# Folding the key weights in sixteen array tiles over 512 columns, put in place by DMAs through DRAM, in a gated mix of linear attention and a feed-forward layer

## The chip, the core and the metric

The kernel runs on one core of one Trainium2 chip. The metric is the device time of one execution in microseconds, the median of several runs. Before the change it is 508.11 us (three runs, 507.98 to 508.29).

## What is computed

One input x (2048 rows of 512) goes through two branches, which a gate mixes row by row. All values are float32.

```python
q, k, v = split(x @ wqkv)                  # 32 heads of 16
pq, pk = q @ w_phi, k @ w_phi              # w_phi: one 16x16 matrix per head
phi_q = [softmax(pq), softmax(-pq)];  phi_k = [softmax(pk), softmax(-pk)]
kv = phi_k^T v;  z = sum(phi_k)            # per head, over all rows
a = (phi_q kv) / (phi_q z + 1e-6) @ wo
b = relu(x @ w1 + b1)^2 @ w2 + b2          # w1: 512x1792
g = sigmoid(sum(x * gate_w))
out = g * a + (1 - g) * b
```

## The kernel before, in words

**Numbers.** Each float32 operand of a large matmul is split into a high part and a low part (`split`, L62: ScalarE copies the high part, L64, VectorE subtracts it for the low one, L67), and a product is three matmuls (`mm3`, L75: L77, L78, L79). So whoever wants a weight needs ScalarE first and VectorE second.

**The feed-forward branch** is the backbone of the order. The 1792 hidden columns are 14 chunks of 128, in two sweeps of seven (0 to 6, 7 to 13); each sweep runs over four blocks of 512 rows. For each chunk an up projection (12 matmuls) fills one PSUM bank `u`; ScalarE does the relu with bias into `r` (L418), the square (L419) and the high part `hh`; VectorE does the low part `hl`; twelve down matmuls add to four banks `d`. There are two buffers for `r`. Four further banks turn round (`bank`, L54): hidden tiles, folds and projections take the one that was used longest ago, and wait until it has been read. Two of them are taken out of the turn later, one for the sums over keys, one for `pX`.

**The attention branch** is laid between these steps. Every function of it has a slot, in half steps: slot 2t is before step t's up projection, 2t + 1 behind it, 2t + 1.5 in the midst of step t's down matmuls (`at`, L782, `run`, L843). The slots fix an order in which the code is recorded; a scheduler then orders the instructions of each engine, by priorities and its own estimates, and from there on every engine works through its row strictly from the front. What it chose is shown by the order of the built program.

**The key weights.** The product wk times w_phi is folded once into one matrix, since pk = x (wk w_phi). w_phi has 32 diagonal blocks of 16, so the fold works in array tiles of 32 by 32: `tiles_fold` (L177) does 64 matmuls over 128 columns (four `g`, four `c`, four row strips `r`) into four PSUM banks, VectorE turns the four banks by 32 by 32 blocks into two tiles `turned` (L196), and ScalarE copies them in 16 pieces to their places in four `raw` tiles (L200; two of them lie in one tile `tmp`), next to the value weights that a DMA has put there (L175). It is called at slot 5.5, in step 2, at the head of the first `joint` piece.

**What uses them.** Keys and values are projected together, with seven products in place of eight (a Strassen scheme over rows and columns). `joint` (L215), in six pieces at slots 5.5 to 11, makes from the `raw` tiles the weights of the products: `operand` (L203) splits one, and VectorE's subtractions (L216) between them make the next. Four are held in SBUF; three go through two slots (`sloto` 0 and 1) or others and are stored to DRAM (`wkeep`, L213) and fetched again later. Slot 0 is written with product 3's weights, stored, and then written with product 1's, which the first `pX` matmul reads at slot 14. `joint_last` (L233) makes the last two weights, `w4`.

**Loads.** SyncE issues the loads in its row; a DMA waits there for its buffer to be free. Eight completion counters turn round, so a DMA also waits for the one eight before it. The stage `in` has four buffers.

Of the kernel before, what the change touches and what calls it, by code (L numbers as in the profile page):

```python
# [8 lines left out]
F32 = mybir.dt.float32  # L9
F32R = mybir.dt.float32r  # L10
AF = mybir.ActivationFunctionType
# [5 lines left out]
P = 128  # L17
S, D, H, DH, F = 2048, 512, 32, 16, 1792
NK = D // P
# [10 lines left out]
AHEAD = 150  # L30
HELD = 2, 4, 5, 7
# [4 lines left out]
def tile_gated_mix(ctx: ExitStack, tc: tile.TileContext, xT, xn, wqT, wkT, wphi, wv, wo, w1, b1, w2, b2, gw, out):  # L36
    nc = tc.nc
# [83 lines left out]
    st, up_w, down_w = {}, {}, {}  # L121
# [9 lines left out]
    nc.gpsimd.memset(kvb, 0.0)  # L131
    part = dram.tile([NB * NC, P, D], F32, name="part")
    wkeep = dram.tile([len(KEPT), 2, P, 2 * D], F32, name="wkeep")
    zrow = dram.tile([2 * D], F32, name="zrow")
    vext = [hold.tile([P, H * VW], F32, tag="vz", name=f"vext{i}") for i in range(NV)]
    heads = lambda v: v.rearrange("p (h v) -> p h v", v=VW)
# [13 lines left out]
    def fold(loaded, nm, k):  # L150
        wph, *t = loaded
        ps = bank(f"fold{nm}{k}")
        for g in range(NK):
            nc.tensor.matmul(ps[:, g * P:(g + 1) * P], t[g][:, k * P:(k + 1) * P], wph[:, g * P:(g + 1) * P],
                             start=True, stop=True)
        hi = wpool.tile([P, 512], F32R, tag=f"wah{k}", name=f"w{nm}h{k}")
        lo = wpool.tile([P, 512], F32R, tag=f"wal{k}", name=f"w{nm}l{k}")
        with tc.high_priority(offset=AHEAD):
            split(ps, hi, lo, nc.scalar, nc.vector)
        return hi, lo  # L160
# [16 lines left out]
    def tiles_fold(loaded):  # L177
        wph, *t = loaded
        pss = [bank(f"fold{r}") for r in range(4)]

        def mm(g, r, c):
            rows, cols = slice(32 * r, 32 * r + 32), slice(32 * c, 32 * c + 32)
            return nc.tensor.matmul(pss[r][cols, g * P:(g + 1) * P],
                                    wph[rows, g * P + 32 * r:g * P + 32 * r + 32],
                                    t[g][rows, :].rearrange("p (k c q) -> p k c q", c=4, q=32)[:, :, c, :],
                                    start=True, stop=True, skip_group_check=True)

        last = None
        for x in [(g, r, c) for g in range(NK) for c in range(4) for r in range(4)]:
            with tc.issue_after(last.ins) if last else nullcontext():  # L190
                last = mm(*x)
        for half in range(2):
            tb = work.tile([P, 2, 4, NK, 32], F32, tag="tb", name="turned", bufs=2)
            for r in range(2):
                with tc.high_priority(offset=AHEAD):
                    st["turned"] = nc.vector.transpose(tb[:, r].rearrange("p g k q -> p (g k q)"), pss[2 * half + r])  # L196
            for k in range(NK):
                dst = st["raw"][k].rearrange("p (h z g r f) -> p h z g r f", h=2, z=2, g=2, r=4)
                for h in range(2):
                    nc.scalar.activation(dst[:, h, 0, :, 2 * half:2 * half + 2],  # L200
                                         tb[:, :, 2 * h:2 * h + 2, k].rearrange("p r g q -> p g r q"), AF.Copy)

    def operand(i, j, src, slot=None, ehi=None, elo=None):  # L203
        if i in HELD:
            w, k = "ab"[i > 4], 2 * (HELD.index(i) % 2) + j
            hi, lo = (wpool.tile([P, 512], F32R, tag=f"w{w}{hl}{k}", name=f"w{i}{j}", bufs=1) for hl in "hl")
# [248 lines left out]
    def do_fold(nm, k):  # L455
        with tc.issue_after(st["up"].ins):
            st["wa", nm, k] = fold(st["wT"], nm, k)
        if k == NK - 1:
            st["wa"] = [st["wa", nm, i] for i in range(NK)]
            if nm == "k":  # L460
                banks.pop()

    def do_joint(j, piece):
        if (j, piece) == (0, 0):
            joint_start(st["wT"])
            with tc.issue_after(st["up"].ins):
                tiles_fold(st["wT"])
        with tc.issue_after(st["up"].ins):
            joint(j, piece)
        if (j, piece) == (1, 0):  # L470
            banks.remove(ps_b)
# [310 lines left out]
    def at(slot, f, *a):  # L782
        steps.setdefault(int(2 * slot) / 2, []).append(lambda: f(*a))

    for fc in range(LAG + 1, NFH):
        if fc > FIRST:
            at(2 * (fc - LAG) - 2, do_w1_first, fc)
        at(2 * (fc - LAG) - (2 if fc == LAG + 1 else 1), do_w2, fc)
    at(0, do_wT, wkT)
    for slot, j, piece in ((5.5, 0, 0), (6, 1, 0), (8, 0, 1), (9, 1, 1), (10, 1, 2), (11, 0, 2)):  # L790
        at(slot, do_joint, j, piece)
    for j in range(2):
# [48 lines left out]
    hid, last = {}, len(work_list) - 1  # L841
# [107 lines left out]
```

## Time and profile before

| what | value |
|---|---|
| median of the runs | 508.11 us (507.98 to 508.29) |
| span of the profiled execution | 506.8 us |
| TensorE busy | 502.0 us, 99% |
| VectorE busy | 405.9 us, 80% |
| ScalarE busy | 256.2 us, 51% |
| GpSimd busy | 88.4 us, 17% |
| DMA | 76.13 MB, 150 GB/s in the mean |
| the fold's matmuls (L183) | start at 27.00 us |
| the fold's four transposes (L196) | start at 28.88 us |
| first `pX` matmul (L647) | 52.31 us |

The span is the time from the first to the last instruction of one execution; the runs' times hold a little more. In a row of the profile, "L77 PE MATMUL d<-w2h,hh 128*128 128x512 f32 x222 | 86.9, 391" is line, engine, operation, tile written and tiles read, shape, count, busy us in all and mean ns of one; behind it stands the idle time of the engine ahead of such instructions, and who ended it. Matmuls overlap in a pipeline: one lasts 390 ns, and the next starts long before its end. L-numbers are those of the kernel before; behind the changed lines the change's numbers are 1 to 6 higher.

### The profile page before, as it was taken

What the parts mean: (1) busy time and instruction counts of PE and PEld (TensorE: products, weight loads), DVE (VectorE), ACT (ScalarE), POOL (GpSimd) and SP (SyncE); (2) the same over time, 40 slices, a digit from 0 to 9 for tenths busy, and PEclk for the clock granted to TensorE, in tenths of its full rate; (3) what the DMA queues carried; (4) which work ended last, traced back from release to release, by engine and by line L of the source; (5) the groups of instructions that cost most, each with busy time, mean ns of one, the idle gap of its engine ahead of it and who ended that gap; (6) DMA issues with size and microseconds to landing.
All of it is one profiled execution on the core that took longest, in us unless ns stands there. A gap on an engine that the chain in (4) does not pass through costs nothing.

```text
span 506.8 us, 9362 instructions
## 1 busy us (share of the span) xinstructions
PE 502.0 (99%) x3522; PEld 406.4 (80%) x3522; DVE 405.9 (80%) x679; ACT 256.2 (51%) x458; POOL 88.4 (17%) x103
## 2 busy tenths in 40 slices
PE   9999999999999999999999999999999999999997
PEld 5878788788888888888888877788787878788776
DVE  5569957998795979796898989897869797897824
ACT  4887655555263474454574745444456354333540
POOL 0000151204420025000013050211222221111200
PEclk9999999999999999999999999999999999999999
DMA  8858587756854578771375221325112231032102
GB/s 262 279 194 284 187 311 219 232 196 231 288 187 158 182 236 308 242 228 65 87 219 195 63 83 43 104 76 147 39 31 88 71 85 43 8 125 63 38 26 84
DMA packets 45861, 76.13 MB, mean 150 GB/s; under 512 B 6904, under 2 KB 23032, under 8 KB 45816
## 3 DMA queue, kind: packets, MB, share of 16 engines
q1 hardware_dynamic: 36104, 41.78, 26.7%
q10 hardware_dynamic: 6768, 23.79, 13.7%
q0 software_dynamic: 2944, 9.96, 5.4%
q8 instruction: 28, 0.46, 0.4%
q14 instruction: 17, 0.14, 0.1%
HBM read 57.68 MB, written 11.54 MB: 137 GB/s over the span
## 4 chain that ended last, share of the span: by engine, by line
PE 90%; DVE 6%; DMA 1%; POOL 1%; ACT 1%; issue 1%; DVEq 0%; POOLq 0%; ACTq 0%
PE d L77 9%; PE d L78 9%; PE d L79 9%; PE u L77 9%; PE u L78 8%; PE u L79 8%; PE pX L647 3%; PE att L79 3%; PE pX L649 3%; PE att L77 3%; PE att L78 3%; PE pX L648 3%; PE q L79 2%; PE q L78 2%; PE q L77 2%; PE pY L647 2%
## 5 line engine op out<-in xcount | busy, mean ns | idle before, releaser
L418 ACT ACTIVATE r<-u,b1c 128x512 f32<-128x512 f32 x56 | 38.5, 688 | 125.5 <-PE u L79 123.6
L77 PE MATMUL d<-w2h,hh 128*128 128x512 f32 x222 | 86.9, 391 | 0.0
L78 PE MATMUL d<-w2l,hh 128*128 128x512 f32 x222 | 86.5, 390 | 0.0
L79 PE MATMUL d<-w2h,hl 128*128 128x512 f32 x222 | 86.4, 389 | 0.0
L77 PE MATMUL u<-xh,w1h 128*128 128x512 f32 x212 | 83.7, 395 | 0.0
L78 PE MATMUL u<-xl,w1h 128*128 128x512 f32 x212 | 82.6, 390 | 0.0
L79 PE MATMUL u<-xh,w1l 128*128 128x512 f32 x212 | 82.5, 389 | 0.0
L333 POOL TENSOR_TENSOR ez<-e,z 128x512 f32<-128x512 f32 x32 | 43.1, 1370 | 166.6 <-ACT e L305 166.6
L67 DVE TENSOR_TENSOR hl<-r,hh 128x512 fp32r<-128x512 f32 x56 | 37.7, 674 | 24.7 <-ACT hh L64 24.7
L77 PEld LDWEIGHTS d<-w2h,hh 128*128 128x128 f32 x222 | 41.7, 188 | 9.2 <-issue 0.6
L78 PEld LDWEIGHTS d<-w2l,hh 128*128 128x128 f32 x222 | 41.7, 188 | 8.9 <-DVE w2l L67 0.4
L77 PEld LDWEIGHTS u<-xh,w1h 128*128 128x128 f32 x212 | 39.8, 188 | 11.1 <-issue 2.9
L79 PEld LDWEIGHTS d<-w2h,hl 128*128 128x128 f32 x222 | 41.7, 188 | 8.7
L79 PEld LDWEIGHTS u<-xh,w1l 128*128 128x128 f32 x212 | 39.8, 188 | 8.6 <-DVE w1l L67 0.2
L78 PEld LDWEIGHTS u<-xl,w1h 128*128 128x128 f32 x212 | 39.8, 188 | 7.9
L305 ACT ACTIVATE e<-e 128x1024 f32<-128x1024 f32 x27 | 28.6, 1059 | 25.2 <-DVE e L303 25.0
L308 DVE TENSOR_REDUCE sm<-e 128x64 f32<-128x1024 f32 x27 | 32.8, 1214 | 10.4 <-ACT e L305 10.4
L64 ACT ACTIVATE hh<-r 128x512 fp32r<-128x512 f32 x56 | 35.2, 628 | 1.1
L419 ACT ACTIVATE r<-r 128x512 f32<-128x512 f32 x56 | 35.0, 624 | 0.7
L686 ACT ACTIVATE tmp<-pX 128x512 f32<-128x512 f32 x24 | 14.4, 598 | 31.2 <-PE pX L649 27.6
L371 ACT ACTIVATE phiT<-tb 32x256 f32<-32x256 f32 x64 | 26.4, 412 | 6.1 <-DVE tb L356 5.1
L340 DVE TENSOR_REDUCE dz<-ez 128x64 f32<-128x1024 f32 x16 | 19.4, 1211 | 11.5 <-POOL ez L333 11.5
(184 smaller groups left out, 985.5 us busy)
## 6 DMA issues: line engine op xcount, KB each, us to landing
sloto<-wkeep ACTq DMA_DIRECT2D x30, 512.0 KB, 4.1
in<-in_xT SPq DMA_DIRECT2D x42, 256.0 KB, 4.2
slotez<-wkeep ACTq DMA_DIRECT2D x15, 512.0 KB, 4.6
phiT<-tb SPq DMA_DIRECT2D x192, 32.0 KB, 1.9
in<-in_w SPq DMA_DIRECT2D x23, 256.0 KB, 3.2
part<-row POOLq DMA_DIRECT2D x16, 256.0 KB, 5.2
row<-part SPq DMA_DIRECT2D x16, 256.0 KB, 2.7
out<-row SPq DMA_DIRECT2D x15, 256.0 KB, 2.2
```

The costliest lines, as they stand in the source:

```text
L64: i = nc.scalar.activation(hi, src, AF.Copy)
L67: st["lo"] = elo.tensor_tensor(lo, src, hi.bitcast(F32), ALU.subtract)
L77: nc.tensor.matmul(o, ah[:, sa], bh[:, sb], start=first, stop=False)
L78: nc.tensor.matmul(o, ah[:, sa], bl[:, sb], start=False, stop=False)
L79: return nc.tensor.matmul(o, al[:, sa], bh[:, sb], start=False, stop=last)
L305: nc.scalar.activation(ef, ef, AF.Exp)
L308: nc.vector.tensor_reduce(sm, e3, AX.X, ALU.add)
L333: nc.gpsimd.tensor_tensor(ez[:, hs, :], e3[:, hs, :], zbc[half], ALU.mult)
L371: nc.scalar.activation(dst, src, AF.Copy)
L418: st["relu"] = nc.scalar.activation(r, ps, AF.Relu, bias=b1c[:, fc:fc + 1])
L419: nc.scalar.activation(r, r, AF.Square)
L647: nc.tensor.matmul(ps, h, wh, start=first and j == 0, stop=False, skip_group_check=True)
```

## The change

The fold takes 16 matmuls instead of 64: for each strip `r` and each `g` one array tile goes over all 512 columns, so that the column strips of the array are now the four `g` and no longer the four `c`. It is called at slot 3.5, in step 1, instead of 5.5 (the value weights' DMAs and the tiles of `joint_start` come there too). VectorE turns the four banks into one tile `turned`, which shares its place in SBUF with the held weights `w4`. ScalarE's 16 copies are gone: four DMAs of 32 partitions each, in pieces of 128 numbers, store the turned tile to a DRAM tensor `wfold`, and four DMAs load it from there into the `raw` tiles. These eight are on SyncE's queue. The held weights of `w4` and the second half of the query weights now lie in one tile (`held`).

```diff
+    wfold = dram.tile([NK, P, D], F32, name="wfold")
...
     def tiles_fold(loaded):
         wph, *t = loaded
         pss = [bank(f"fold{r}") for r in range(4)]
-        def mm(g, r, c):
-            rows, cols = slice(32 * r, 32 * r + 32), slice(32 * c, 32 * c + 32)
-            return nc.tensor.matmul(pss[r][cols, g * P:(g + 1) * P],
-                                    wph[rows, g * P + 32 * r:g * P + 32 * r + 32],
-                                    t[g][rows, :].rearrange("p (k c q) -> p k c q", c=4, q=32)[:, :, c, :],
-                                    start=True, stop=True, skip_group_check=True)
-        last = None
-        for x in [(g, r, c) for g in range(NK) for c in range(4) for r in range(4)]:
-            with tc.issue_after(last.ins) if last else nullcontext():
-                last = mm(*x)
-        for half in range(2):
-            tb = work.tile([P, 2, 4, NK, 32], F32, tag="tb", name="turned", bufs=2)
-            for r in range(2):
-                with tc.high_priority(offset=AHEAD):
-                    st["turned"] = nc.vector.transpose(tb[:, r].rearrange("p g k q -> p (g k q)"), pss[2 * half + r])
-            for k in range(NK):
-                dst = st["raw"][k].rearrange("p (h z g r f) -> p h z g r f", h=2, z=2, g=2, r=4)
-                for h in range(2):
-                    nc.scalar.activation(dst[:, h, 0, :, 2 * half:2 * half + 2],
-                                         tb[:, :, 2 * h:2 * h + 2, k].rearrange("p r g q -> p g r q"), AF.Copy)
+        for g in range(NK):
+            for r in range(4):
+                rows = slice(32 * r, 32 * r + 32)
+                with tc.issue_after(st["up"].ins):
+                    st["up"] = nc.tensor.matmul(pss[r][32 * g:32 * g + 32, :],
+                                                wph[rows, g * P + 32 * r:g * P + 32 * r + 32], t[g][rows, :],
+                                                start=True, stop=True, skip_group_check=True)
+        tb = wpool.tile([P, 4 * NK, 4, 32], F32, tag="wa23", name="turned", bufs=1)
+        for r in range(4):
+            with tc.high_priority(offset=AHEAD):
+                st["turned"] = nc.vector.transpose(tb[:, :, r, :], pss[r].rearrange("p (k q) -> p k q", q=32))
+        to = wfold.rearrange("t (c q) (g f) -> g q (t c) f", c=4, g=NK)
+        for g in range(NK):
+            nc.sync.dma_start(to[g], tb[32 * g:32 * g + 32].rearrange("p k r f -> p k (r f)"))
+        for k in (0, 2, 1, 3):
+            nc.sync.dma_start(st["raw"][k].rearrange("p (h c) -> p h c", h=2)[:, :, :256],
+                                wfold[k].rearrange("p (h c) -> p h c", h=2))
...
+    def held(k):
+        if k < 2:
+            return [wpool.tile([P, 512], F32R, tag=f"wa{hl}{k}", name=f"wa{hl}{k}", bufs=1) for hl in "hl"]
+        if k == 2:
+            st["wa23"] = wpool.tile([P, 4, 512], F32R, tag="wa23", name="wa23", bufs=1)
+        return [st["wa23"][:, 2 * (k - 2) + i, :] for i in range(2)]
...
+    def key_fold():
+        joint_start(st["wT"])
+        tiles_fold(st["wT"])
+
     def do_joint(j, piece):
-        if (j, piece) == (0, 0):
-            joint_start(st["wT"])
-            with tc.issue_after(st["up"].ins):
-                tiles_fold(st["wT"])
...
     at(0, do_wT, wkT)
+    at(3.5, key_fold)
```

The scheduler answers with another order on every engine up to about 100 us; from there on the orders are alike. Three places of it follow. In the names, `w1l4` is the low part of w1's chunk 4, `xl1_0` that of x, block 1, first quarter.

On VectorE, around the transposes, before:

```order
L67 TENSOR_TENSOR w1l4_325<-in_322,w1h4_324 128x512
L67 TENSOR_TENSOR hl_303<-r_299,hh_302 128x512
L67 TENSOR_TENSOR w2l4_333<-in_330,w2h4_332 128x512
L67 TENSOR_TENSOR w1l5_351<-in_348,w1h5_350 128x512
L67 TENSOR_TENSOR hl_379<-r_375,hh_378 128x512
L196 STREAM_TRANSPOSE turned_472<-fold0_404 128x512
L196 STREAM_TRANSPOSE turned_472<-fold1_405 128x512
```

And now:

```order
L67 TENSOR_TENSOR w1l4_326<-in_323,w1h4_325 128x512
L67 TENSOR_TENSOR hl_304<-r_300,hh_303 128x512
L67 TENSOR_TENSOR w2l4_334<-in_331,w2h4_333 128x512
L190 STREAM_TRANSPOSE turned_373<-fold0_353 128x16x32
L190 STREAM_TRANSPOSE turned_373<-fold1_354 128x16x32
L190 STREAM_TRANSPOSE turned_373<-fold3_356 128x16x32
L190 STREAM_TRANSPOSE turned_373<-fold2_355 128x16x32
L67 TENSOR_TENSOR w1l5_395<-in_392,w1h5_394 128x512
L67 TENSOR_TENSOR hl_423<-r_419,hh_422 128x512
```

The transposes moved ahead of w1's chunk 5 and of the low part of chunk 4's hidden tile. On TensorE the fold now stands six matmuls ahead of chunk 4's up projection, which takes the bank of `fold0`.

On ScalarE, around the relu of block 0's chunk 6 (`r_606` before, `r_550` now), the second write of slot 0 (`sloto0` from `raw0`) and w2's chunk 6, before:

```order
L64 ACTIVATE sloto0_395<-raw0_398 128x512
L418 ACTIVATE r_606<-u_591,b1c_101 128x512
L64 ACTIVATE w2h6_556<-in_554 128x512
L64 ACTIVATE sloto1_396<-tmp_394 128x512
L419 ACTIVATE r_606<-r_606 128x512
```

And now, with the splits of the folded weights (products 3 and 2) ahead and the relu of block 1's chunk 0 (`r_603`) behind it:

```order
L64 ACTIVATE sloto0_344<-raw2_349 128x512
L64 ACTIVATE wah0_530<-raw2_349 128x512
L64 ACTIVATE sloto1_345<-tmp_343 128x512
L64 ACTIVATE wah1_561<-tmp_343 128x512
L423 ACTIVATE r_550<-u_535,b1c_101 128x512
L423 ACTIVATE r_603<-u_589,b1c_101 128x512
L64 ACTIVATE w2h6_500<-in_498 128x512
L424 ACTIVATE r_550<-r_550 128x512
L64 ACTIVATE sloto0_344<-raw0_347 128x512
L64 ACTIVATE hh_553<-r_550 128x512
```

The relu moved ahead of slot 0's second write. VectorE's row has the low parts of these weights in the same order (slot 0, product 2, slot 1, product 2, w2's chunk 6, slot 0 again) and then 15 operations up to and with the low part `hl` of block 1's chunk 0, among them `joint`'s subtractions.

On TensorE, behind the up projection of block 1's chunk 2 (`u_763` before, `u_707` now). `u_837` is chunk 3, `pX_753` and `pY_791` are the split products of the scan, before:

```order
L79 MATMUL u_763<-xh1_3_572,w1l2_135 128x512
L647 MATMUL pY_791<-w20_586,xh1_2_560 128x512
L648 MATMUL pY_791<-w20_587,xh1_2_560 128x512
L649 MATMUL pY_791<-w20_586,xl1_2_561 128x512
L647 MATMUL pY_791<-w21_617,xh1_3_572 128x512
L648 MATMUL pY_791<-w21_618,xh1_3_572 128x512
L649 MATMUL pY_791<-w21_617,xl1_3_573 128x512
L77 MATMUL u_837<-xh1_0_526,w1h3_227 128x512
L647 MATMUL pX_753<-slotez_397,sh_725 128x512
L648 MATMUL pX_753<-slotez_397,sh_725 128x512
```

And now, where `u_778` is chunk 3 and `u_876` chunk 4 (the lines of dots stand for the rest of the six products of `pY` and of the twelve matmuls of chunk 3):

```order
L79 MATMUL u_707<-xh1_3_516,w1l2_136 128x512
L652 MATMUL pY_732<-wah0_530,xh1_2_504 128x512
...
L654 MATMUL pY_732<-wah1_561,xl1_3_517 128x512
L77 MATMUL u_778<-xh1_0_470,w1h3_228 128x512
...
L79 MATMUL u_778<-xh1_3_516,w1l3_229 128x512
L77 MATMUL u_876<-xh1_0_470,w1h4_325 128x512
L78 MATMUL u_876<-xl1_0_471,w1h4_325 128x512
L79 MATMUL u_876<-xh1_0_470,w1l4_326 128x512
L652 MATMUL pX_697<-slotez_346,sh_669 128x512
```

Before, chunk 3 gave way to `pX` after its first matmul. Now all twelve matmuls of chunk 3 and the first three of chunk 4 stand ahead of `pX`; `u_778` takes the PSUM bank that `u_707` had, and `u_876` takes it from `u_778`.

More of the change, by code (lines that the diff above doesn't have):

```diff
@@ L155, in fold @@
                              start=True, stop=True)
-        hi = wpool.tile([P, 512], F32R, tag=f"wah{k}", name=f"w{nm}h{k}")
-        lo = wpool.tile([P, 512], F32R, tag=f"wal{k}", name=f"w{nm}l{k}")
+        hi, lo = held(k)
         with tc.high_priority(offset=AHEAD):
@@ L203, in operand @@
+    def held(k):
[4 more added lines that the diff above has]
+        return [st["wa23"][:, 2 * (k - 2) + i, :] for i in range(2)]
     def operand(i, j, src, slot=None, ehi=None, elo=None):
         if i in HELD:
-            w, k = "ab"[i > 4], 2 * (HELD.index(i) % 2) + j
-            hi, lo = (wpool.tile([P, 512], F32R, tag=f"w{w}{hl}{k}", name=f"w{i}{j}", bufs=1) for hl in "hl")
+            k = 2 * (HELD.index(i) % 2) + j
+            if i > 4:
+                hi, lo = (wpool.tile([P, 512], F32R, tag=f"wb{hl}{k}", name=f"w{i}{j}", bufs=1) for hl in "hl")
+            else:
+                hi, lo = held(k)
```

## The prediction

> **What bounds the kernel now.** I read the page's heads first, then the busy time by stretches from 20 to 60 us, then TensorE's timeline around the fold.
>
> ```profile
> span 506.8 us, 9362 instructions
> PE 502.0 (99%) x3522; PEld 406.4 (80%) x3522; DVE 405.9 (80%) x679; ACT 256.2 (51%) x458; POOL 88.4 (17%) x103
> PEclk9999999999999999999999999999999999999999
> PE 90%; DVE 6%; DMA 1%; POOL 1%; ACT 1%; issue 1%; DVEq 0%; POOLq 0%; ACTq 0%
> ```
>
> TensorE is busy for 502.0 of 506.8 us at the full clock and holds 90% of the chain that ended last. The stretches below (PE, PEld, DVE, ACT, POOL busy time in 5 us each) say the same of the place that the change touches, and one thing more: VectorE has 2.3 us free between 30 and 35 us, and none between 45 and 55.
>
> ```profile
> 30.00:35.00 5.00, 5.00 (x24) 4.14 (x23) 2.66 (x6) 4.65 (x19) 0.00 (x0) 1.00 0.41 151
> 35.00:40.00 5.00, 5.00 (x23) 3.79 (x22) 4.90 (x9) 4.56 (x9) 1.24 (x2) 1.00 0.56 194
> 45.00:50.00 5.00, 5.00 (x23) 4.14 (x23) 5.00 (x9) 3.99 (x8) 0.02 (x1) 1.00 0.79 279
> 50.00:55.00 5.00, 5.00 (x23) 4.14 (x23) 5.00 (x11) 3.53 (x6) 1.06 (x2) 1.00 0.27 108
> ```
>
> TensorE's timeline (start, duration), with the fold in its midst and, for a price, one numerator step:
>
> ```profile
> 22.82 0.39 PE L77 MATMUL u<-xh,w1h 128*128 128x512 f32 x1
> 25.32 0.39 PE L79 MATMUL u<-xh,w1l 128*128 128x512 f32 x1
> ...
> 26.68 0.39 PE L79 MATMUL d<-w2h,hl 128*128 128x512 f32 x1
> 27.00 1.90 PE L183 MATMUL fold<-row 32*32 32x128 f32 x128
> 28.83 0.50 PE L77 MATMUL d<-w2h,hh 128*128 128x512 f32 x1
> 29.16 0.40 PE L78 MATMUL d<-w2l,hh 128*128 128x512 f32 x1
> ...
> 298.43 1.09 PE L382 MATMUL num<-phiT,kvb 64*32 64x256 f32 x32
> 299.45 0.50 PE L77 MATMUL u<-xh,w1h 128*128 128x512 f32 x1
> ```
>
> From 22.82 to 26.68 are 17 steps: a full matmul starts every 0.227 us and lasts 0.39. So the end moves by what TensorE has less to do, and by every wait that the change puts into its row. The span of this execution is 506.8, the median of the runs 508.11: 1.3 us lie around the span, and I add changes to the median. One microsecond is 0.2%, about what a measurement of this kernel can tell from no change.
>
> **The fold itself (A).** Now it starts 0.09 late (26.68 + 0.23 = 26.91 against 27.00), holds the row until 28.83, and the matmul behind takes 0.33 instead of 0.23. The 0.2 us of these two switches stay. The 64 matmuls show 128 records, two passes each; the change has 16 with 32 passes of 512 columns. The nearest row is the numerator: 32 passes too, of 256 columns, eight tiles at once, so four rounds of 256 columns, in 299.45 - 298.43 = 1.02 us. Sixteen tiles at once make two rounds of 512, as many columns one after another: 1.02, and a little for the eight more starts, 1.06. A = 1.06 - 1.83 = -0.8. Its bounds are 0 (as many columns in all as now, so no gain) and -0.8. [...]
>
> **ScalarE's copies.** They go, and ScalarE is no bound here, so 16 copies of 0.29 taken off it give nothing by themselves.
>
> ```profile
> L200 ACT ACTIVATE raw<-turned x8: 293/294/310, 30.2 to 32.9; 128x128 f32<-128x128 f32 x8
> L200 ACT ACTIVATE tmp<-turned x8: 293/294/300, 30.6 to 34.1; 128x128 f32<-128x128 f32 x8
> ```
>
> **The first tile behind the fold (B).** The fold takes all four turning PSUM banks; the hidden tile of chunk 4 stands six matmuls behind it and takes the bank of the fold's first tile. Before, chunk 4 started at 22.82; with the fold ahead of it, it could at 22.82 + 1.06 + 0.2 = 24.1. The bank is free when VectorE has turned that tile, and VectorE comes to it behind the low parts of w1 chunk 4, hl and w2 chunk 4, the last at 23.26:
>
> ```profile
> 23.26 0.68 DVE L67 TENSOR_TENSOR w2l<-in,w2h 128x512 fp32r<-128x512 f32 x1
> 28.88 2.51 DVE L196 STREAM_TRANSPOSE turned<-fold 128x512 f32<-128x512 f32 x4 [0.40 <-PE fold L183]
> ...
> 47.72 0.68 DVE L216 TENSOR_TENSOR raw<-raw,raw 128x512 f32<-128x512 f32 x1
> 48.32 1.29 DVE L67 TENSOR_TENSOR w<-tmp,w 128x512 fp32r<-128x512 f32 x2
> 49.53 0.68 DVE L216 TENSOR_TENSOR tmp<-tmp 128x512 f32<-128x512 f32 x1
> ```
>
> VectorE starts such an operation every 0.60 (47.72, 48.32, two of them, 49.53). So the first transpose runs 23.86 to 24.55, chunk 4 starts at 24.6, and a matmul after a stop costs 0.1 more, as at 28.83. B = +0.6, 0.3 to 0.8. The turned tiles written with gaps I price as now, 0.6 each.
>
> **The way through DRAM.** The four transposes end at 24.6 - 0.7 + 2.5 = 26.4; SyncE then issues four stores, chunk 3 of x for block 1, w2 chunk 5 and w1 chunk 6, and only then, when all stores have landed, four loads. No row shows this trip. Its bounds are two landings, each between a lone and a crowded one:
>
> ```profile
> in<-in_xT SPq DMA_DIRECT2D x4, 256.0 KB, 5.7
> wkeep<-sloto POOLq DMA_DIRECT2D x4, 512.0 KB, 4.8
> in<-in_w SPq DMA_DIRECT2D x3, 256.0 KB, 2.8
> ```
>
> The x loads of 512-byte pieces are the like of the stores. With 0.9 for each of three more transfers on either leg (my choice between the two lengths over four transfers) the last load lands between 26.4 + 2 x (2.8 + 2.7) = 37 and 26.4 + 2 x (5.7 + 2.7) = 43; I take 39, since ScalarE and VectorE can't use it sooner anyway: they do the splits of x, w2 chunk 5 and w1 chunk 6 first. The four splits of the folded weights behind it are done by about 41. What they are needed for comes at 47 (next part), so the trip is hidden as long as it lands by 43 or so: the store of the first slot's weights, 4.8 more, must be in before ScalarE overwrites that slot at 49.2.
>
> **The new order (C).** This is the term that decides. Before, the up projection of chunk 6 of block 0 ran ahead of block 1's, and its relu stood behind the second write of slot 0 on ScalarE. Now it runs behind most of those of chunks 0 and 1 of block 1, and the relu stands ahead of that write. From chunk 4's start (24.6 + 0.1) to its last matmul are 96 steps: 24.7 + 96 x 0.227 = 46.5, ended at 46.9. ScalarE's row has after the four splits this chunk's relu, so ScalarE stands from 41 to 46.9. Behind it are a second relu, w2 chunk 6, a square, and slot 0's second write.
>
> ```profile
> 25.74 0.69 ACT L418 ACTIVATE r<-u,b1c 128x512 f32<-128x512 f32 x1 [0.55 <-PE u L79]
> ...
> 45.60 0.67 ACT L418 ACTIVATE r<-u,b1c 128x512 f32<-128x512 f32 x1
> 46.17 0.62 ACT L64 ACTIVATE w<-tmp 128x512 fp32r<-128x512 f32 x1
> 46.69 0.62 ACT L419 ACTIVATE r<-r 128x512 f32<-128x512 f32 x1
> ```
>
> A relu starts with the end of its last matmul (25.32 + 0.39 = 25.71, start 25.74) and takes 0.57 of the row, others 0.52. So: relus at 46.9 and 47.5, w2 chunk 6 from 48.1 to 48.7, square 48.6, slot 0 from 49.15 to 49.8. VectorE's next operation needs that w2 chunk 6, so VectorE has nothing to do from 41.4 to 48.8, and this is the time (45 to 55) in which it had none to spare. Then come w2's low part, slot 0's low part at 49.8, and 15 more before the end of "hl" of block 1's chunk 0: it starts at 49.8 + 15 x 0.60 = 58.8 and ends at 59.5. The buffer r that it reads is the one that the relu of chunk 2 must write, which empties the only PSUM bank that the next hidden tile, chunk 3, can take. That relu: 59.55 to 60.25. Chunk 3 starts at 60.3, plus 0.1 after the stop. TensorE would have been there 144 steps after chunk 4's start: 24.7 + 144 x 0.227 = 57.4. C = +2.9 + 0.1 = +3.0, with 2.4 to 3.5 for half a microsecond of gaps either way. Nothing is late before: the pX matmul that needs slot 0 comes 16 steps, 3.6 us, after the chunk's last start, at 50.1; slot 0 is written at 49.8.
>
> **Behind it (D, E).** Before, the two hidden tiles had six pY matmuls between them and then pX:
>
> ```profile
> 56.16 0.39 PE L79 MATMUL u<-xh,w1l 128*128 128x512 f32 x1
> ...
> 57.75 0.39 PE L77 MATMUL u<-xh,w1h 128*128 128x512 f32 x1
> 57.98 0.50 PE L647 MATMUL pX<-slotez,sh 128*128 128x512 f32 x1
> 58.32 0.40 PE L648 MATMUL pX<-slotez,sh 128*128 128x512 f32 x1
> ```
>
> Now chunk 4 of block 1 follows chunk 3 at once and in the same bank, so the whole turn stands in the open: the last matmul of chunk 3 starts at 60.4 + 11 x 0.227 = 62.9 and ends at 63.3, the relu at 64.0, chunk 4 at 64.05 against 63.1. D = +1.0 (0.9 to 1.2). E: pX waited 0.1 at 57.98 for the split sums; these still stand behind the same backlog of VectorE: +0.3 (0 to 0.5). Later TensorE is behind by four microseconds and everything else has that much more time; no wait before 300 us is long enough to give it back. The query weights use the same four pieces of SBUF and the same instructions: nothing.
>
> Sum: -0.8 + 0.6 + 3.0 + 1.0 + 0.3 = +4.1. I take 508.1 + 4.1 = 512.2. The ends of the terms give -0.8 + 0.3 + 2.4 + 0.9 + 0 = +2.8 and 0 + 0.8 + 3.5 + 1.2 + 0.5 = +6.0: 510.9 to 514.1.
>
> **Rivals.** (1) Not slower: VectorE's backlog doesn't come last. Place: chunk 3 of block 1. If "hl" of chunk 0 ends before 56.6, 2.9 us sooner than worked out, C is gone, and -0.8 + 0.6 + 1.0 is left: 508.9, no change; were the banks of B and D free as well, 507.3, still within 0.2%. For it: VectorE has 2.3 us free at 30 to 35. Against: that is before the wait, and the operations behind it each show 0.60. 0.10. (2) The trip through DRAM is late, beyond 43 us: ScalarE then waits at slot 0, and each microsecond moves the whole of C. With 45 it would be two more: 514.2. For it: 5.7 at the crowded hour; against: the DMA engines' busy share (the last column but one) is 0.41 and 0.56 from 30 to 40. 0.08. (3) The change doesn't do what it says: sixteen tiles of 512 columns do not run at once, and the fold gets longer. One after the other, 32 passes at the numerator's 0.5 for 512 columns (1.02 for four rounds of 256) would be 16 us, and the time some 527; the fold's 128 passes in 1.83 speak against it. 0.02.
>
> **How the numbers follow.** The forecast has 0.80 and the likeliest time, 512.2; its own range is 510.9 to 514.1, the ends of the terms. To hold the time 8 times in 10 I reach a little into rival (2) and as far down: 510.7 to 514.5. Slower by over 0.2%: the forecast, (2) and (3), 0.90. Of rival (1) both times lie within 0.2%, 0.06; the rest of its 0.10, 0.04, I leave to faster, for what a bound of a term may have missed.
>
> **What would show it.** Right: 32 fold passes from about 21.5 lasting 1.1; a first stop of TensorE of half a microsecond at 24; ScalarE waiting some 6 us for a hidden tile up to 47; VectorE idle 41 to 48.8; TensorE's stops at 57 to 60 of 3 us, at 63 of 1 us, each in front of a hidden tile, put down to a relu; no stop of more than a tenth for the loads out of DRAM. Wrong: a stop in front of pX at 50 put down to a DMA (rival 2), or TensorE without a gap from 55 to 65 (rival 1).

## The result, and the profile after

The changed kernel takes 515.02 us (median of four runs, 513.77 to 515.5) against 508.08: a ratio of 1.0133, with a 95% interval of 1.0121 to 1.0145. It is slower by 1.3%. The forecast was 512.2, the range 510.7 to 514.5: the direction was right, the size too small. The profiled execution has a span of 513.7 us against 506.8, so 6.9 us are to be accounted for.

The page's head after the change:

```profile
span 513.7 us, 9173 instructions
PE 503.7 (98%) x3426; PEld 405.9 (79%) x3426; DVE 405.6 (79%) x679; ACT 253.3 (49%) x442; POOL 87.7 (17%) x103
PEclk9999899999999999999999999999999999999999
```

TensorE has less to do than before, and yet its busy time is 1.7 us longer; one slice of its clock, from 51 to 64 us, shows an 8. Both belong together, as will be seen. TensorE's waits behind its first microseconds (who waited for whom: us in all, times, longest); before, TensorE waited 0.2 us in all once it had started:

```profile
PE u L77 <- ACT r L423: 3.6, 2, 2.8
...
PE pX L652 <- DMA sloto<-wkeep: 1.0, 2, 0.7
PE u L77 <- DVE turned L190: 0.4, 1, 0.4
PE u L79 <- issue: 0.3, 1, 0.3
```

The places on TensorE's timeline (start, duration, in brackets the idle time before and who ended it):

```profile
21.59 1.14 PE L184 MATMUL fold<-row 32*32 32x512 f32 x32
22.66 0.50 PE L77 MATMUL d<-w2h,hh 128*128 128x512 f32 x1
...
24.72 0.47 PE L77 MATMUL u<-xh,w1h 128*128 128x512 f32 x1 [0.41 <-DVE turned L190]
...
57.24 0.39 PE L654 MATMUL pY<-wah,xl 128*128 128x512 f32 x1
60.44 0.50 PE L77 MATMUL u<-xh,w1h 128*128 128x512 f32 x1 [2.81 <-ACT r L423]
...
61.48 0.63 PE L78 MATMUL u<-xl,w1h 128*128 128x512 f32 x1
61.90 0.63 PE L79 MATMUL u<-xh,w1l 128*128 128x512 f32 x1
...
64.46 0.59 PE L79 MATMUL u<-xh,w1l 128*128 128x512 f32 x1
65.83 0.50 PE L77 MATMUL u<-xh,w1h 128*128 128x512 f32 x1 [0.78 <-ACT r L423]
...
75.23 0.47 PE L652 MATMUL pX<-sloto,sh 128*128 128x512 f32 x1 [0.27 <-DMA sloto<-wkeep]
...
81.66 0.50 PE L652 MATMUL pX<-sloto,xh 128*128 128x512 f32 x1 [0.74 <-DMA sloto<-wkeep]
```

The fold holds the row for 1.07 us (21.59 to 22.66; before, 1.83). Chunk 4 waits for a bank at 24.7, chunk 3 of block 1 starts at 60.44, the next hidden tile at 65.83. Between 61.48 and 64.46 something is new: a matmul starts every 0.43 us instead of 0.227. The window from 60 to 65 us names it, the last three columns being the granted clock, the DMA engines' share and GB/s:

```profile
60.00:65.00 5.00, 4.57 (x12) 3.16 (x12) 5.00 (x15) 2.86 (x6) 0.53 (x1) 0.66 0.79 298
```

The clock is 0.66 in this stretch. The chain in front of the long stop, first on ScalarE, then on VectorE:

```profile
41.72 0.61 ACT L64 ACTIVATE wah<-tmp 128x512 fp32r<-128x512 f32 x1
47.01 1.27 ACT L423 ACTIVATE r<-u,b1c 128x512 f32<-128x512 f32 x2 [4.68 <-PE u L79]
...
49.21 0.62 ACT L64 ACTIVATE sloto<-raw 128x512 fp32r<-128x512 f32 x1
...
59.70 0.69 ACT L423 ACTIVATE r<-u,b1c 128x512 f32<-128x512 f32 x1 [0.64 <-DVE hl L67]
```

```profile
48.83 0.69 DVE L67 TENSOR_TENSOR w2l<-in,w2h 128x512 fp32r<-128x512 f32 x1 [5.69 <-ACT w2h L64]
49.87 0.69 DVE L67 TENSOR_TENSOR sloto<-raw,sloto 128x512 fp32r<-128x512 f32 x1 [0.34 <-ACT sloto L64]
...
58.91 0.69 DVE L67 TENSOR_TENSOR hl<-r,hh 128x512 fp32r<-128x512 f32 x1
```

ScalarE stands 4.68 us in front of chunk 6's relu, VectorE 5.69 us behind that, slot 0 is written at 49.2, and the low part `hl` of block 1's chunk 0 ends at 59.6, the relu that empties the bank starts at 59.7. That is the chain that was forecast, to 0.2 us at each link.

The account, from step to step of TensorE's timeline (what a step takes beyond 0.227), in us:

| place | forecast | measured |
|---|---|---|
| A, the fold | -0.8 | 1.07 - 1.83 = -0.76 |
| B, the first tile behind it, 23.92 to 25.03 | +0.6 | +0.66 |
| C, the stop before chunk 3, 57.24 to 60.77 | +3.0 | +3.08 |
| D, the turn of the bank, 64.46 to 66.16, at full clock | +1.0 | +1.05 |
| E, pX behind it | +0.3 | 0 |
| seven steps at half clock and the last one's longer end | not forecast | 8 x 0.20 = +1.6 |
| two stops of pX for a slot's reload, 74.57 and 80.53 | not forecast | 0.51 + 1.02 = +1.53 |
| small switches and stops that one kernel has: 0.6 after, at 146 us, 0.9 before | - | -0.3 |
| sum | +4.1 | +6.9 |

So the forecast terms come to 4.0 and the two new ones to 3.1.

### The profile page after: what moved, and what is told of

It is laid out like the page before. It is cut to its first block, busy times and chain, and to the rows that moved or that the text cites. A ratio compares the mean times of both kernels' runs of the same rounds, so it can differ in the third digit from the quotient of the medians.

```text
span 513.7 us, 9173 instructions
## 1 busy us (share of the span) xinstructions
PE 503.7 (98%) x3426; PEld 405.9 (79%) x3426; DVE 405.6 (79%) x679; ACT 253.3 (49%) x442; POOL 87.7 (17%) x103
## 4 chain that ended last, share of the span: by engine, by line
PE 85%; DVE 7%; DMA 3%; ACT 2%; issue 1%; POOL 1%; SPq 0%; DVEq 0%; ACTq 0%; POOLq 0%
PE u L77 9%; PE u L79 8%; PE u L78 8%; PE d L77 8%; PE d L78 8%; PE d L79 8%; PE pX L652 3%; PE att L79 3%; PE att L78 3%; PE att L77 3%; PE pX L654 3%; PE pX L653 3%; DMA sloto<-wkeep 2%; PE q L78 2%; PE q L77 2%; PE q L79 2%
```

## The experiments

Every kernel was timed in five rounds beside the kernel before (508.4 to 508.5 us on those chips). The changed kernel itself, timed again as x9, gave a ratio of 1.0148 there with runs from 513.5 to 517.9: two versions that differ by 0.3% are not told apart by their medians, so what is read below is mostly the place of the stops, each from one profiled execution.

| run | median us | ratio, 95% interval |
|---|---|---|
| x1_relu_back | 513.28 | 1.0100 (1.0077 to 1.0122) |
| x2_fill_stop | 515.08 | 1.0130 (1.0108 to 1.0152) |
| x3_fold_slot15 | 513.76 | 1.0109 (1.0081 to 1.0137) |
| x4_own_r | 518.19 | 1.0185 (1.0164 to 1.0207) |
| x5_before_slot35 | 514.13 | 1.0116 (1.0102 to 1.0130) |
| x6_other_slot | 518.89 | 1.0201 (1.0163 to 1.0239) |
| x7_all_early | 512.61 | 1.0091 (1.0065 to 1.0117) |
| x8_fold_slot55 | 519.37 | 1.0223 (1.0194 to 1.0253) |
| x9_changed_again | 516.24 | 1.0148 (1.0123 to 1.0173) |
| x10_no_trip | 519.06 | 1.0210 (1.0178 to 1.0243) |
| x11_later_loads | 516.98 | 1.0159 (1.0140 to 1.0179) |
| x12_fill_twelve | 515.39 | 1.0144 (1.0123 to 1.0165) |

The ratio and interval of x6 leave out its longest execution, 524.06 us.

### What makes the stop before chunk 3

**x1: chunk 6's relu behind slot 0's second write again.** The edit, in `hidden` and `joint`, where `"hi"` is ScalarE's copy of the last split:

```diff
             operand(1, j, a, j)
+            st["again", j] = st["hi"]
...
+        first = fc == NFH - 1 and ("again", 0) in st and "past" not in st
...
-        with tc.high_priority(offset=AHEAD):
+        with tc.high_priority(offset=AHEAD), tc.issue_after(st["again", 0].ins) if first else nullcontext():
             st["relu"] = nc.scalar.activation(r, ps, AF.Relu, bias=b1c[:, fc:fc + 1])
```

> ScalarE's relu of block 0's chunk 6 stands behind slot 0's second write again; nothing else is asked for. Theory (the order of ScalarE's row makes VectorE idle from 42 to 49 us, and its backlog is the stop of 2.8 us in front of chunk 3): slot 0 is written when its store has landed, 45 to 46 us instead of 49.2, VectorE's idle time shrinks to about 3 us, the stop in front of chunk 3 falls from 2.8 to under 1, the half clock behind it goes too; of the 6.9 us that were lost, 3 to 6 come back: 509 to 512. Rival (the weights come out of DRAM too late, whatever the order): the loads land as before, at 39 to 42, the stop stays over 2 us, and the time stays at 514 to 515.

ScalarE, then TensorE, then the store of slot 0 issued at 40.6 us (a view of the tile `wkeep` in that window; the time from issue to landing):

```profile
47.35 0.63 ACT L64 ACTIVATE sloto<-raw 128x512 fp32r<-128x512 f32 x1 [4.46 <-issue]
47.89 1.25 ACT L427 ACTIVATE r<-u,b1c 128x512 f32<-128x512 f32 x2
```

```profile
59.26 0.50 PE L77 MATMUL u<-xh,w1h 128*128 128x512 f32 x1 [1.62 <-ACT r L427]
...
80.06 0.50 PE L656 MATMUL pX<-sloto,xh 128*128 128x512 f32 x1 [2.13 <-DMA sloto<-wkeep]
```

```profile
DMA to landing us min/median/max: 6.7/6.7/6.7
```

The write moved ahead of the relu, but only from 49.2 to 47.35: what it waits for now is its own slot, whose weights were split late (the folded weights were there at 38.9) and whose store took 6.7 us, 40.6 + 6.7 = 47.3. (The profile puts this wait down to "issue"; that it was the store is read from the two times.) The stop fell from 2.81 to 1.62, and the clock stayed full behind it; the reload's stop grew to 2.13. So the theory holds in part: the relu was the first limit, and the late weights with their store a second one 1.9 us behind it. The expected "3 to 6 come back" was too much: the ratio fell from 1.0133 to 1.0100, which is 1.7 us.

**x6: the second limit away too.** Product 3's first weights go through the third slot, so slot 0 waits for no store:

```diff
-            operand(3, j, d, j)
+            operand(3, j, d, j or 2)
```

> The changed kernel, but product 3's first weights go through the third slot (slotez) instead of slot 0, so that the second write of slot 0 has no store of 6.7 us to wait for; the scheduler then also puts that write ahead of chunk 6's relu. Theory (two limits stood one behind the other at slot 0's second write, the relu at 49.2 and the store of the late weights at 47.4): slot 0 is written by 44 us, the stop before chunk 3 is under 0.5 and the half clock goes; a hidden tile's turn behind it stays, 1 to 2.2: 509.5 to 512. Rival (VectorE's work between 50 and 62 us is too much in this order however early slot 0 is written): a stop of over 1.5 us before chunk 3 or pX stays, 513 to 515.

ScalarE writes slot 0 with product 1 at 39.2 us:

```profile
39.16 0.63 ACT L64 ACTIVATE sloto<-raw 128x512 fp32r<-128x512 f32 x1
```

There is no stop in front of chunk 3. But chunk 4 behind it waits 1.8, and then the reloads 4.9 in two stops, and a pY product 2.9, with a clock of 0.57 from 85 to 90 us, behind the longer reload, and of 0.66 from 115 to 120, behind the product. VectorE still stands idle, 4.93 us up to 49.6, and the relu in front of chunk 4 waits for an `hl` of its backlog. The profiled execution is the longest of the six (524.06; the others 516.15 to 522.69), so its later stops need not stand in the others. The first half of the theory held; that nothing would take the stop's place did not, and the time lies above what the theory and the rival expected.

**x4: a buffer of its own for chunk 2's relu** (the tenth hidden tile in the program's order).

```diff
-        r = work.tile([P, SB], F32, tag="r", name="r")
+        st["n"] = st.get("n", -1) + 1
+        r = row() if st["n"] == 9 else work.tile([P, SB], F32, tag="r", name="r")
```

> The relu of block 1's chunk 2 writes a buffer of its own (one of the row tiles) and needn't wait for the low part of chunk 0; the second write of slot 0 stays behind chunk 6's relu. Theory (VectorE's backlog is what is late, the buffer only its first victim): the stop in front of chunk 3 goes, and TensorE stops instead for the split sums of pX, which stand behind the same backlog, by 2 to 7 us: 514 to 518. Rival (the shared r buffer is the cause): stop and half clock go and nothing takes their place: 509 to 510.

```profile
58.11 0.39 PE L655 MATMUL pY<-wah,xl 128*128 128x512 f32 x1
65.31 0.79 PE L653 MATMUL pX<-slotez,sh 128*128 128x512 f32 x1 [6.81 <-ACT sh L64]
```

The link from `hl` to the relu is cut, and TensorE stops for 6.81 us in front of pX instead, for the split sums that stand behind the same backlog. VectorE works from 50.7 to 65 us without a gap, and the sums are made at 64 us. This is what the theory said: the shared buffer is the first victim, VectorE's backlog is the cause. One thing is not shown by x4: in its order pX stands ahead of chunk 3, which comes only at 70.75, so whether chunk 3 would have run without a stop can't be seen.

### The clock behind the stop

**x2 and x12: filling the stop.** Thirteen (x2) and twelve (x12) matmuls of zeros follow the first pY product, so that TensorE has something to do; they add zero. All other rows are the changed kernel's, but for the memset of the zeros on GpSimd.

```diff
...
-            nc.tensor.matmul(ps, l, wh, start=False, stop=j == 1, skip_group_check=True)
+            fill = j == 1 and (p, i) == (0, 2)
+            e = nc.tensor.matmul(ps, l, wh, start=False, stop=j == 1 and not fill, skip_group_check=True)
+        if fill:
+            for n in range(12):
+                with tc.issue_after(e.ins):
+                    e = nc.tensor.matmul(ps.rearrange("p (a b) -> p a b", a=4), quiet, quiet.unsqueeze(1).to_broadcast([P, 4, P]), start=False, stop=n == 12 - 1, skip_group_check=True)
+            st["fill"] = e
```

> Thirteen matmuls of a zero weight tile over 512 zero columns, added to the pY bank, stand on TensorE where it stops in front of chunk 3 (they add zero); every other row is as in the changed kernel. Theory (TensorE's clock halves because it stood still for 2.8 us): the stop is filled, chunk 3 starts at the same 60.4, the granted clock stays at 1.00 between 60 and 65 us, and the eight steps of 0.43 us are 0.23: 1.6 us less in every run, 513 to 513.5 against 514.8. Rival (the clock falls for another reason): the clock is 0.66 there as before, and the time is the changed kernel's, 514 to 515.5.

> As x2_fill_stop with twelve zero matmuls, so that the filling ends before the relu has emptied the bank. Theory: mean clock 1.000 in every run, no step of 0.43 us behind chunk 3; the runs lie where those runs of the changed kernel lie whose clock is 1.000, 1 to 2 us below its runs at 0.997: 512.5 to 514.5. Rival: runs at 0.997 as in the changed kernel.

x12's timeline, and its window:

```profile
57.45 2.76 PE L662 MATMUL pY<-quiet 128*128 128x512 bf16 x12
60.41 0.50 PE L77 MATMUL u<-xh,w1h 128*128 128x512 f32 x1 [0.20 <-ACT r L425]
...
61.92 0.39 PE L77 MATMUL u<-xh,w1h 128*128 128x512 f32 x1
```

```profile
60.00:65.00 5.00, 4.02 (x16) 2.83 (x16) 5.00 (x15) 4.31 (x9) 0.53 (x1) 1.00 0.81 305
```

Chunk 3 starts when it started before, and behind it no step is slow. Of ten executions of x2 and x12 nine have a mean clock of 0.999 or more. The changed kernel's own ten (the first four and x9's six) have two of that kind, and eight at 0.997 or less. That the standstill costs the clock is shown by this. In the medians the 1.6 us do not show (515.39 against x9's 516.24, intervals that overlap), and both kernels lie above what was expected. The bank wait at 24 us and the reloads vary by as much: in x2's profile the first was 1.2 us instead of 0.4, as a load of w2 came later.

**x9: the changed kernel again.**

> The changed kernel itself, beside the next three. Theory (the clock halves in some executions and not in others, as the stop falls against the clock's own window): runs with a mean clock of 0.997 lie 1 to 2 us above runs with 1.000; 513.5 to 515.5.

The runs do not fall into two groups as expected: 513.53 has a clock of 0.997 and 515.27 one of 0.999. The profile shows why the clock alone does not sort them. Here the stop before chunk 3 was again 2.8 us and left the clock at 1.00; another one halved it:

```profile
79.39 0.39 PE L654 MATMUL pX<-sloto,xl 128*128 128x512 f32 x1
81.74 0.50 PE L652 MATMUL pX<-sloto,xh 128*128 128x512 f32 x1 [1.96 <-DMA sloto<-wkeep]
```

A stop of 1.96 us was enough here, one of 2.8 was not, and in x1 stops of 1.62 and 2.13 were not. All stops of 2.9 us or more in these runs were followed by a slow stretch: 6.81 us in x4 (a clock of 0.60 from 65 to 70 us), 3.56 in x5 and 6.27 in x8 (a matmul every 0.43 us behind them), 3.7 and 2.9 in x6 (0.57 from 85 to 90 and 0.66 from 115 to 120), 2.96 in x7 (0.69 from 55 to 60), 4.58 in x10 (0.50 from 50 to 55). The first profile's stretch lasted from 61.45 to 64.87, 3.4 us, this one from 83.05 to 86.46, 3.4 as well.

The clock records of the traces say what the length of a stop does not. The first profile runs at full clock for 54.61 us, 16 times 3.413, from 6.84 us up to its slow stretch, and x9 for 78.51, 23 times 3.413, from 4.54. The kernel before runs at full clock for 501.76 us, 147 times 3.413, from 6.95. So in these three the clock changes on a grid of 3.41 us, which starts at another time in each. These are windows on that grid, counted back from the slow stretch, of the first profile (one row) and of x9 (four rows); the second number is TensorE's busy time, the last but two the clock:

```profile
58.04:61.45 3.41, 1.01 (x4) 0.86 (x5) 3.41 (x7) 2.35 (x4) 1.07 (x2) 1.00 0.31 129
```

```profile
55.74:59.15 3.41, 1.49 (x7) 0.91 (x5) 3.41 (x8) 1.37 (x3) 0.25 (x1) 1.00 0.00 0
59.15:62.57 3.42, 2.53 (x11) 2.11 (x12) 3.42 (x10) 2.71 (x6) 0.81 (x2) 1.00 0.71 287
79.63:83.05 3.42, 1.47 (x7) 1.09 (x7) 3.25 (x6) 0.31 (x1) 0.23 (x1) 1.00 0.97 345
83.05:86.46 3.41, 3.41 (x10) 2.65 (x9) 0.00 (x0) 1.84 (x4) 0.83 (x2) 0.50 0.72 216
```

The first profile's stop puts 2.40 of its 2.81 us into one window. The stop of the same length in x9 is cut by an edge into 1.92 and 0.89, and the stop of 1.96 lies whole in one. In the fourteen profiles, up to the last matmul, each of the nine windows at full clock with 1.96 us or more of standstill is followed by a slow one, and none with 1.54 or less is; in between, 1.62 (x7) is followed and 1.92 (x9) is not, so the bound itself is not read off here.

### The reload of the slots

**x11: block 2's loads two slots later, their splits one and a half.**

```diff
-        s, late = ((4, 2), (19.5, 1), (22, 2.5), (36, 2))[b]
+        s, late = ((4, 2), (21.5, .5), (22, 2.5), (36, 2))[b]
```

> The loads of block 2's x on GpSimd's queue are called two slots later (21.5 instead of 19.5), so that they no longer share the DMA engines with the reload of slot 1 at 76 us; up to there all is as in the changed kernel. Theory (the reload's 5.2 us to landing come of that sharing, and the row leaves it 4.6): it lands in under 4.5, the stop of 0.9 before pX at 80.5 goes: 0.5 to 1.2 less than the changed kernel beside it. Rival (the reload is slow by itself): the stop stays as it is.

Before the change, slot 1's reload is issued at 68.5 us and used 6.6 us later; its landing takes 3.2. In the changed row fewer matmuls stand between the slot's last use and its next: it is issued at 76.2 and would be used 4.6 us later, at 80.76, and lands after 5.4 in the first profile and 6.7 in x9's. In x11 it is issued at 76.2 again and lands after 4.5, the view of `wkeep` says:

```profile
DMA to landing us min/median/max: 4.5/4.5/4.5
```

```profile
80.58 0.39 PE L654 MATMUL pX<-sloto,xl 128*128 128x512 f32 x1
80.80 0.49 PE L652 MATMUL pX<-sloto,xh 128*128 128x512 f32 x1
```

The second stop is gone, as expected, if only just: the reload lands at 80.75 and is wanted at 80.80. That reload was late because it shared the DMA engines with block 2's loads (5.4 us with them beside it in the first profile, 4.5 in x11 without), and because the new row leaves it 4.6 instead of 6.6 us. The first stop, at 75.28, stays with 0.68; its own reload, issued at 68.1, took 7.1 us to land. The median did not fall (516.98 against 516.24), and in the profiled execution the stop at 146 us grew from 0.33 to 1.5.

### The place and the way

Two things changed together: the fold stands two steps earlier, and its result goes through DRAM. **x5** has the first without the second (the kernel before, its fold called at 3.5), **x8** the second without the first (the changed kernel, its fold called at 5.5).

```diff
...
+    at(3.5, key_fold)
```

> The kernel before, whole, with its own fold (64 matmuls, ScalarE's copies, no DRAM) called at slot 3.5 instead of 5.5. Theory now (the way through DRAM brings the weights 4 to 7 us later than ScalarE's copies did, and the splits, stores and slot writes chain behind it; where the fold stands in the program matters little): raw is written by 30 us, VectorE has no idle stretch from 42 to 49, no stop before chunk 3; at most one wait for a bank or buffer of about 1 us: 507.5 to 510. Rival (calling the fold two slots earlier lets the scheduler choose a bad order, whichever way the weights go): 512 or more, with a stop of over 1.5 us between 55 and 65 us.

```diff
-    at(3.5, key_fold)
+    at(5.5, key_fold)
```

> The changed kernel with its fold called at slot 5.5, where it stood before the change. Theory (the trip through DRAM is the cost, and slot 3.5 hides two thirds of it): the fold runs 5 us later, the weights land at 43 to 47, slot 0's writes and VectorE's backlog are later by as much, TensorE stops for 6 to 10 us between 48 and 72 us and its clock halves for a while: 518 to 524. Rival (the place is what costs): not above the changed kernel's 514.8, since the order is nearer to that of before.

TensorE's waits in x5, all of them, then VectorE's row at the fold:

```profile
PE u L77 <- DVE turned L196: 3.6, 1, 3.6
PE u L77 <- ACT w1h L64: 1.4, 1, 1.4
PE warm L494 <- DVE zeros L488: 1.2, 1, 1.2
```

```profile
26.81 0.69 DVE L67 TENSOR_TENSOR w1l<-in,w1h 128x512 fp32r<-128x512 f32 x1 [2.85 <-ACT w1h L64]
27.42 2.50 DVE L196 STREAM_TRANSPOSE turned<-fold 128x512 f32<-128x512 f32 x4
```

And in x8, in front of a hidden tile:

```profile
68.54 0.80 PE L77 MATMUL u<-xh,w1h 128*128 128x512 f32 x1 [6.27 <-ACT r L423]
```

x5 is nearly as slow as the changed kernel, which the rival said; but it has no stop at all behind 45 us, neither before chunk 3 nor at a reload. Its loss is at the fold, where the transposes stand on VectorE behind the low part of a w1 chunk whose load is late, and TensorE waits 3.56 us for their bank; the clock halves behind that (a matmul every 0.43 us from 29.86 to 32.85), and at 42 us a w1 chunk is late by another 1.4. x8, in which ScalarE has the first weights out of DRAM at 45.2 us instead of 38.7, has its stop at the same kind of place as the changed kernel, 6.27 instead of 2.81, as expected. So the stop before the hidden tiles goes with the way through DRAM, and the early place has a price of its own that the change mostly escaped (B, 0.66). x8 and the kernel before also differ in the fold's matmuls and in ScalarE's copies; x10 takes away the wait for the trip alone.

**x10: an early fold whose weights wait for no store.** The folded half is read from the value weights instead, so the fold is left out of the result.

```diff
-                                wfold[k].rearrange("p (h c) -> p h c", h=2))
+                                wv[k * P:(k + 1) * P, :].rearrange("p (h c) -> p h c", h=2))
```

> The four loads of the folded weights read the value weights' tensor instead of wfold, so they wait for no store: the folded half of the weights is left out of the result, while fold, transposes, stores and loads all still run. Theory (the trip is the cause: it makes the weights late, and the scheduler, which reckons with it, puts the relu ahead): weights in raw by 33 us, no stop of more than 0.5 before chunk 3, no half clock there, no reload wait over 0.5 between 70 and 85; what remains is at most 4 us of waits around 42 to 45, where splits of x stand behind splits of weights: 508 to 512.5. Rival (an early fold makes a bad order whichever way the weights come): a stop of over 2 us between 55 and 66 us, 514 or more.

```profile
47.65 1.22 PE L77 MATMUL u<-xh,w1h 128*128 128x512 f32 x2 [4.58 <-ACT xh L64]
50.08 0.79 PE L78 MATMUL u<-xl,w1h 128*128 128x512 f32 x1 [1.21 <-DVE xl L67]
```

```profile
39.64 0.63 ACT L64 ACTIVATE sloto<-tmp 128x512 fp32r<-128x512 f32 x1 [3.87 <-DMA wkeep<-sloto]
...
46.99 1.13 ACT L64 ACTIVATE xh<-in 128x512 fp32r<-128x512 f32 x2
```

No stop before chunk 3, as expected, but a worse one earlier: the scheduler now lets the weights go first, and block 1's last pieces of x are split at 47 us, behind ten other things and a store; the clock is at half from 45.5 to 55.7 (0.55 in the stretch from 45 to 50 us, 0.50 from 50 to 55). The expected 508 to 512.5 was wrong, 519.06 was measured. The trip is therefore not a cost that can be lifted off by itself: the order is made with it in mind, and another order has its stop elsewhere.

**x3 and x7: the fold earlier still.** x3 calls it at slot 1.5, x7 does that with x1's and x6's edits.

```diff
-    at(3.5, key_fold)
+    at(1.5, key_fold)
```

> The fold is called at slot 1.5 instead of 3.5. In this order slot 0's second write stands four instructions ahead of the relu of chunk 6 on ScalarE, as before the change. Theory: no backlog of VectorE, so no stop in front of chunk 3 and no half clock; what stays is the fold's gain of 0.8 against the bank waits around the fold (0.6 each for one or two tiles) and the turn of chunk 4 behind chunk 3 (1.0): 508.5 to 510.5. Rival (the trip through DRAM or the bank waits carry the loss): 513 or more.

> The changed kernel with the fold at slot 1.5 and product 3's first weights in the third slot: everything that the runs so far say is late comes earlier. Theory: waits of 0.6 each for fold banks and a low part, one of 0.7 in front of a down product, and the reload of a slot (0.9 to 2.3 in the runs so far) against the fold's gain of 0.8: 508.5 to 511. Rival: 512 or more, as with the fold at slot 1.5 alone.

ScalarE in x3, then TensorE in x7:

```profile
49.52 0.63 ACT L64 ACTIVATE sloto<-tmp 128x512 fp32r<-128x512 f32 x1 [2.07 <-DMA wkeep<-sloto]
```

```profile
52.85 0.50 PE L77 MATMUL u<-xh,w1h 128*128 128x512 f32 x1 [2.96 <-ACT r L427]
```

Neither stops before chunk 3. x3 waits 2.2 us before the first pX, whose bank a relu empties that stands behind the rewriting of slot 1, and that waits for its store; x7 waits 2.96 for a hidden tile at about the same time, and its clock is 0.69 from 55 to 60 us in the profiled execution. Both times lie above what their theories expected, x3 by 3.3 us and x7 by 1.6. x7's six executions show the price of the clock once more: four with a mean clock of 1.000 took 510.82 to 512.92, two with 0.997 took 514.56 and 515.89. x7 is the best version found, still 0.9% slower than the kernel before; nothing here points to one that beats it, as the fold's gain is 0.76 us in all.

## Why the prediction was wrong

**A, right.** The pack, 32 passes for 16 matmuls, takes 1.07 us; 1.06 was taken from the numerator's row.

**B, D, right:** 0.66 against 0.6, 1.05 against 1.0, with the waits put down to the transposes and to a relu as said. In other runs TensorE waited up to 1.6 us there (x6), more than B's bound of 0.8: the transposes stand behind a low part that waits for a load.

**The way through DRAM, right in what it costs here, too kind in its margin.** The first weights were split at 38.7 and the last at 41.2; 39 was taken. It is hidden because the relu holds ScalarE until 47. x1 shows that without the relu the first store, 6.7 us there instead of the 4.8 taken, holds slot 0 until 47.35. "Hidden as long as it lands by 43 or so" was said with that store at 4.8; in the changed kernel it took 7.1, from 40.5 to 47.6, so the margin to slot 0's write at 49.2 was 1.6 us, and the trip was the next thing to be late.

**C, right in place, chain and length, wrong in price.** Relus at 46.9 (47.01), VectorE idle until 48.8 (48.83), slot 0 at 49.15 (49.21), `hl` ended at 59.5 (59.60), chunk 3 at 60.3 (60.44). The failed step is the sentence "Chunk 3 starts at 60.3, plus 0.1 after the stop", which takes a stop to cost its own length. TensorE stood still for 2.81 us, and its clock then halved for 3.4 us: +1.6. x12 shows that with the same start and no standstill the clock stays (1.00 from 60 to 65 us instead of 0.66). Nothing in the trace of before could show it, since TensorE never stood there. By these runs a stop of 3 us is worth a term with a chance: of the changed kernel's first four executions three have a mean clock of 0.997 and one of 1.000.

**The second failed step** is "Later TensorE is behind by four microseconds and everything else has that much more time". True of work that runs by its own row, false of a DMA that TensorE itself releases: a slot's reload is issued when TensorE has read the slot (the last read ends at 68.48 us before and at 76.16 now, the reload is issued at 68.52 and 76.19), so it is late by as much as TensorE. What counts is the distance between last use and next use in TensorE's row. For the second stop it was 6.6 us before and 4.6 now, against a landing of 3.2 to 6.7, and x11 shows that an earlier landing takes this stop away; what made the first one was not taken apart. The two cost 1.5. The order of the program held the shorter distance already; the prediction followed that order only as far as pX's first product. E, 0.3, did not come.

**Rivals.** "Not slower" fell: VectorE's backlog did come last. "The trip is late" did not happen here and was one step away. The time lies above the range because the upper bounds of the terms, +6.0, held neither of the two missing ones.

**Open.** The stop of 0.33 us at 146.2, put down to "issue", is in most of these orders and not in the kernel before; what it is was not tried. Whether an order exists in which the trip costs nothing is open: a fixed order with and without the trip could not be had, since the scheduler's order changes with each edit.

## What to carry to other kernels

On an engine without a gap, price a stop by what it sets off and not by its length alone: the clock behind it, and each DMA that the stopped engine itself releases. Where a scheduler sets the order, an edit that makes one operand late moves everything that the scheduler thinks is late; read the whole order between the edit and the point where the rows agree again, above all the distance between a buffer's last use and its next. A change that saves 0.8 us on the bound engine isn't worth a longer way for the data, unless that way ends well before the next thing that waits.

## What was not expected of the hardware

The granted clock can halve for 3.4 us after a standstill of as little as 1.96 us (x9), and can stay full after one of 2.8 (x9 too), as the stop falls on a grid of 3.41 us; behind the seven stops of 2.9 and more in these profiles it always fell. A store of 512 KB from SBUF to DRAM, issued at 40 us into this kernel, took 6.7 (x1) to 7.1 us (first profile) to land, where the median of such stores before was 4.8, and slot 1's reload of the same size took 3.2 before and 4.5 (x11) to 6.7 (x9) after.
